# Scoring the end keys of a block-sparse attention step in 32-query tiles

## The chip, the cores and the metric

The kernel runs on one core of a Trainium2 chip. The metric is the device time of one execution in microseconds; for the kernel before it is known from three runs.

## What is computed

Two stages are joined. The first is attention over 4 batches, 8 heads, 768 positions and 64 dimensions, in blocks of 32 positions. A query block sees its own block and the two neighbours, the first and the last block of the sequence (the *end keys*), and three blocks drawn at random for it; the queries of the first and the last block see everything. In the reference:

```
mask = np.abs(blk_i - blk_j) <= window
mask = mask | (blk_i == 0) | (blk_j == 0) | (blk_i == n_blocks - 1) | (blk_j == n_blocks - 1)
for qb in range(n_blocks):
    for kb in sampled_blocks[qb]:
        mask[qb * block:(qb + 1) * block, kb * block:(kb + 1) * block] = True
```

Softmax over the masked scores and the product with the values follow. The second stage is a mixture of 8 experts with noisy top-2 routing: each of the 3072 rows goes through two experts, `relu(x @ w1) @ w2`, weighted by the gate.

## The kernel before, in words

Attention runs as a list of steps (`Attention.macros`). Two batches lie together (`bb`), two heads of a pair lie on the two halves of the 128 partitions (`a`), and a step takes one batch, four heads (two head pairs `r` times `a`) and 128 queries. There are 40 G steps (four ordinary query blocks of 32 in each: 2 batch pairs, 5 units, 4 steps a unit) and, for the queries of the first and last block and the two blocks left over, 8 X steps and 16 D steps. A G step has 256 keys for each query block `j`: 96 sampled keys and 96 neighbours (the *windows*, one matmul of 192 columns for each `j`), and 64 end keys between them.

`Attention.scores` (line 207) gives these to TensorE. The operands are fp32, and each fp32 matmul appears in the trace as two passes, each with a weight load. For each head pair `r`, lines 227 to 229 score the end keys of all 128 queries at once: for each `a` one matmul on a tile of 64 rows by 128 columns (64 by 64 in an X step), 64 columns moving. Lines 230 to 239 then score the windows: for each `j` and `a` one matmul on a tile of 64 rows by 32 columns, 192 columns moving. So a G step issues 8 instructions of the first kind and 32 of the second, an X step 8 and 16. Every result goes to the PSUM tile `s`.

The order on TensorE is fixed in `steps` (line 433). In step n: scores of n; transposes of n-1 (line 299); router work on rows that are done (`turn` line 544, `logits` line 556, and others) at three spots; the product with the values of step n-2 (`av`, line 314, 64 instructions on tiles of 128 by 32). VectorE takes the maximum of the scores (`top`, line 246) and the negative bias `nb` (line 265), ScalarE the exponentials (line 287).

The sampled keys come by GpSimd: `gather_k` (line 205) copies 12 blocks of 32 columns out of the resident keys, for one batch of a unit, two steps before their first use. In the same queue stand the gathers of the sampled values, `gather_v` (line 189, an indirect DMA), each behind a small copy to `tick` (line 417) that waits for VectorE's latest maximum. The neighbouring values come by ScalarE's queue (line 182). Instructions are read from memory by DMA queues of their own.

Of the kernel before, what the change touches and what calls it, by code (L numbers as in the profile page):

```python
# [18 lines left out]
P = 128  # L19
# [19 lines left out]
class Attention:  # L39
# [167 lines left out]
    def scores(self, m):  # L207
        kind, k, bb, h, kh = m
        nc = self.nc
        hpair, g = self.units[k]  # L210
        S = self.st["s", m] = self.ps_s.tile([P, 2, 512], F32, name="s")
        q, KT = self.st["q", k][:, bb], self.KT[hpair][:, bb]
        f = self.first(g)
        hp = lambda a: slice(64 * a, 64 * a + 64)
        mm = lambda out, l, r, pos: nc.tensor.matmul(out, l, r, start=True, stop=True, tile_position=pos)  # L215
        if kind == "D":
            for r in range(2):
                for a in range(2):
                    pr, o = 2 * h + r, 64 * (1 - r)
                    mm(S[o:o + 64, a, 0:384], q[hp(a), pr, 64:P], KT[hp(a), pr, 384 * kh:384 * kh + 384], (64 * a, o))  # L220
            return
        own = self.kv[hpair][:, bb * self.BW:(bb + 1) * self.BW]
        ends = lambda x, n: x.rearrange("p (n c) -> p n c", c=32)[:, 0:n:n - 1, :]
        for r in range(2):
            pr = 2 * h + r
            col, js, o0, n = (256 * r, range(4), 0, P) if kind == "G" else (0, range(2), 64 * r, 64)
            for a in range(2):
                out = S[o0:o0 + n, a, col + 96:col + 160].rearrange("p (n c) -> p n c", c=32)
                mm(out, q[hp(a), pr, 0:n], ends(KT[hp(a), pr], self.NB), (64 * a, o0))
            for j in js:  # L230
                for a in range(2):
                    o = o0 + 32 * j
                    at = own[hp(a), (j * self.PR + pr) * 96:]
                    win = self.GW + pr * self.S + 32 * (f + j - 1)
                    rhs = bass.AP(tensor=at.tensor, offset=at.offset,
                                  ap=[list(at.ap[0]), [win - (j * self.PR + pr) * 96, 2], [1, 96]])
                    out = S[o:o + 32, a, col:col + 256].rearrange("p (n c) -> p n c", c=32)
                    out = bass.AP(tensor=out.tensor, offset=out.offset, ap=[list(out.ap[0]), [160, 2], [1, 96]])
                    mm(out, q[hp(a), pr, 32 * j:32 * j + 32], rhs, (64 * a, o))
# [1111 lines left out]
```

## Time and profile before

| | |
|---|---|
| median of three runs | 897.31 us |
| lowest, highest | 894.2, 899.99 us |
| profiled execution, first to last instruction | 898.7 us |
| mean granted TensorE clock | 0.983 |
| attention's matmuls | 8.5 to about 323 us |
| experts | from 323.95 us |

The profile is of one execution on the chip; its span is in the third line of the table, and no other time is shown for that execution. A busy TensorE is not TensorE at its peak: matmuls overlap, and their ends are modelled. Idle time is printed with what ended it; "issue" means that the engine waited for nothing that the profile shows. Rows that give a stretch list, for each engine, busy microseconds and the number of instructions, then the granted clock, the DMA share and GB/s.

### The profile page before, as it was taken

Reading aid. Unit: us, or ns where it says so; the run is one execution under the profiler, and the core shown is the slowest. Engines: PE = TensorE matmul, PEld = TensorE weight load, DVE = VectorE, ACT = ScalarE, POOL = GpSimd, SP = SyncE. Lnnn points to the kernel's source line nnn. Section 1 sums busy time; section 2 is a strip of 40 time slices with the busy share of each in tenths; the row PEclk is TensorE's granted clock in tenths of the full one; section 3 lists DMA queues with packets and bytes.
Section 4 is the critical chain, followed back from the end, with each engine's and each line's share of the span. In section 5 each row is a group of like instructions: output and inputs, shape, how many; then the busy total and the mean of one; then the engine's idle time right before and its main releaser. Section 6 shows DMA issues by size and latency. Waiting matters only on the chain.

```text
span 898.7 us, 21745 instructions
## 1 busy us (share of the span) xinstructions
PE 827.7 (92%) x9033; PEld 491.8 (55%) x9033; DVE 404.9 (45%) x924; ACT 295.2 (33%) x570; POOL 299.9 (33%) x550
## 2 busy tenths in 40 slices
PE   4999889898996897989999999999999999999993
PEld 2667656766675675465545545545545545545541
DVE  3545557567567557413343343343343343342420
ACT  2565545454565443112212312212212302311300
POOL 2545444441344400233423423413423423424020
PEclk9999999999998899999999999999999999999997
DMA  8856796792568868393952943962952942943011
GB/s 338 297 179 210 228 277 200 284 316 67 153 173 229 215 180 308 123 215 73 221 204 76 266 137 65 199 224 65 217 205 74 268 160 65 270 141 101 9 37 38
DMA packets 122618, 159.70 MB, mean 178 GB/s; under 512 B 66581, under 2 KB 83221, under 8 KB 122512
## 3 DMA queue, kind: packets, MB, share of 16 engines
q1 hardware_dynamic: 96400, 75.76, 31.3%
q0 software_dynamic: 17616, 57.47, 22.1%
q10 hardware_dynamic: 8496, 25.01, 8.9%
q8 instruction: 73, 1.20, 0.6%
q14 instruction: 33, 0.27, 0.1%
HBM read 117.30 MB, written 27.10 MB: 161 GB/s over the span
## 4 chain that ended last, share of the span: by engine, by line
PE 52%; DMA 3%; issue 2%; DVE 0%; POOL 0%; SPq 0%; POOLq 0%
PE ph L891 27%; PE py L913 22%; PE py L924 2%; DMA out_dram<-y,mt 2%; DMA xtb<-xg 1%; DMA xg<-x_rows,gi 0%; PE py L933 0%; POOL out_dram L964 0%; SPq L846 0%; DVE y L962 0%; DVE y L958 0%; PE pr L945 0%; DVE o_ex L1057 0%; POOLq L980 0%; POOLq L964 0%
## 5 line engine op out<-in xcount | busy, mean ns | idle before, releaser
L896 ACT ACTIVATE hh<-ph 128x408 f16<-128x408 f32 (+2 forms) x136 | 66.6, 492 | 368.1 <-PE ph L891 271.7
L964 POOL DMA_INDIRECT out_dram<-y,mt x56 | 61.5, 1098 | 340.6 <-DVE y L958 149.1
L913 PE MATMUL py<-w2h,hh 128*128 128x512 f16 x384 | 145.6, 379 | 0.0
L913 PE MATMUL py<-w2l,hh 128*128 128x512 f16 x384 | 145.5, 379 | 0.0
L913 PE MATMUL py<-w2h,hl 128*128 128x512 f16 x384 | 145.5, 379 | 0.0
L897 DVE SCALAR_TENSOR_TENSOR hl<-ph,hh 128x408 f16<-128x408 f32 (+2 forms) x136 | 75.9, 560 | 153.4 <-ACT hh L896 133.0
L215 PE MATMUL s<-kv,q 64*32 64x192 f32 (+3 forms) x1920 | 114.1, 349 | 20.4 <-DMA kv<-in_k_dram 8.5
L913 PEld LDWEIGHTS <-hh 128*128 128x128 f16 x768 | 74.5, 98 | 90.2 <-issue 2.5
L891 PE MATMUL ph<-xta,w1hb 128*128 128x408 f16 x512 | 109.4, 336 | 0.8 <-issue 0.8
L958 DVE SCALAR_TENSOR_TENSOR y<-py,r_tab,pv 128x512 f32<-128x512 f32 (+1 forms) x49 | 36.7, 750 | 152.0 <-PE py L913 146.6
L891 PE MATMUL ph<-xtb,w1ha 128*128 128x408 f16 (+1 forms) x448 | 93.4, 329 | 5.5 <-DMA xtb<-xg 4.2
L301 ACT ACTIVATE t<-t 128x512 f32<-128x512 f32 (+1 forms) x120 | 62.6, 566 | 96.3 <-PE t L299 93.7
L215 PEld LDWEIGHTS s<-kv,q 64*32 64x32 f32 (+2 forms) x1920 | 53.2, 124 | 60.9 <-issue 32.3
L205 POOL COPY kv<-kv 128x128 f32 x264 | 67.2, 301 | 52.9 <-issue 22.1
L891 PEld LDWEIGHTS <-w1ha 128*128 128x128 f16 x576 | 56.7, 99 | 44.0 <-issue 5.8
L830 POOL DMA_INDIRECT xg<-x_rows,gi x56 | 62.1, 1109 | 51.4 <-DVE gi L816 35.8
L287 ACT ACTIVATE p<-s,nb 128x256 f32<-128x256 f32 x176 | 69.4, 476 | 19.8 <-DVE nb L265 14.6
L246 DVE TENSOR_REDUCE nm<-s 128x4 f32<-128x1024 f32 (+1 forms) x48 | 54.4, 1133 | 44.1 <-PE s L215 34.0
L891 PEld LDWEIGHTS <-w1hb 128*128 128x128 f16 x512 | 50.1, 98 | 39.3 <-issue 1.1
L299 PE MATMUL t<-ident,p 128*128 128x128 f32 x448 | 66.2, 290 | 2.1 <-ACT t L301 2.1
L891 PE MATMUL ph<-xta,w1lb 128*128 128x408 f16 x256 | 65.1, 336 | 0.0
L299 PEld LDWEIGHTS t<-ident,p 128*128 128x128 f32 x448 | 50.1, 145 | 24.7 <-issue 16.4
(176 smaller groups left out, 1013.7 us busy)
## 6 DMA issues: line engine op xcount, KB each, us to landing
wraw<-in_moe_w_dram SPq DMA_DIRECT2D x64, 512.0 KB
vb<-in_v_windows_dram ACTq DMA_DIRECT2D x28, 390.0 KB
vb<-in_v_windows_dram ACTq DMA_DIRECT2D x14, 520.0 KB
kv<-in_v_dram SPq DMA_DIRECT2D x4, 1560.0 KB
q<-in_q_dram SPq DMA_DIRECT2D x12, 512.0 KB
kv<-in_k_dram SPq DMA_DIRECT2D x8, 768.0 KB
out_dram<-zero ACTq DMA_DIRECT2D x8, 768.0 KB
x_rows<-x SPq DMA_DIRECT2D x20, 256.0 KB
```

The lines of the kernel that those rows point to most:

```text
L205: nc.gpsimd.tensor_copy(KG[:, j, :, 32 * s:32 * s + 32], KT[:, :, bass.ds(offs[3 * j + s], 32)])
L215: mm = lambda out, l, r, pos: nc.tensor.matmul(out, l, r, start=True, stop=True, tile_position=pos)
L246: red = lambda out, x: nc.vector.tensor_reduce(out, x, axis=AX.X, op=ALU.max, negate=True)
L287: self.nc.scalar.activation(p[:, 256 * u:256 * u + 256], S[:, a, 256 * r:256 * r + 256], AF.Exp, bias=nb[:, u:u + 1], scale=0.125)
L299: self.nc.tensor.transpose(T[i][:, c:c + P], p[:, i * w + c:i * w + c + P], self.ident)
L301: self.nc.scalar.activation(t[:, i * w:(i + 1) * w], T[i][:, 0:w], AF.Copy)
L830: g = nc.gpsimd.indirect_dma_start(out=self.xg[0:m, c], out_offset=None, in_=self.x_dram[0:nr], in_offset=bass.IndirectOffsetOnAxis(ap=r[" ...
L891: nc.tensor.matmul(ph[:, b, 0:m], w[wt][:, kb, fs], r["xt"][:, kb, a, o:o + m], start=i == 0, stop=i == last)
L896: nc.scalar.activation(hv, ph[:, b, 0:m], AF.Relu)
L897: nc.vector.scalar_tensor_tensor(self.hl[:, f, o:o + m], ph[:, b, 0:m], 0.0, hv, op0=ALU.max, op1=ALU.subtract)
L913: nc.tensor.matmul(py, h[:, f, o], w[x][:, f, :], start=i == 0, stop=i == last)
L964: nc.gpsimd.indirect_dma_start(out=self.out, out_offset=bass.IndirectOffsetOnAxis(ap=r["mt"][0:m, c:c + 1], axis=0), in_=y[0:m], in_offset ...
```

## The change

The end keys of a step are scored for each block of 32 queries by itself: for each `j` and `a` one matmul on a tile of 64 rows by 32 columns, with 64 columns moving, into the same places of `s`. The shape of the tile is that of the windows' matmuls, which follow unchanged. A G step's end keys take 32 instructions on 8 tiles for both pairs together where there were 8 on 2 (4 and 16 for each pair), an X step's 16 where there were 8; the weight loads are as many again.

```
-            col, js, o0, n = (256 * r, range(4), 0, P) if kind == "G" else (0, range(2), 64 * r, 64)
-            for a in range(2):
-                out = S[o0:o0 + n, a, col + 96:col + 160].rearrange("p (n c) -> p n c", c=32)
-                mm(out, q[hp(a), pr, 0:n], ends(KT[hp(a), pr], self.NB), (64 * a, o0))
+            col, js, o0 = (256 * r, range(4), 0) if kind == "G" else (0, range(2), 64 * r)
+            for j in js:
+                o = o0 + 32 * j
+                for a in range(2):
+                    out = S[o:o + 32, a, col + 96:col + 160].rearrange("p (n c) -> p n c", c=32)
+                    mm(out, q[hp(a), pr, 32 * j:32 * j + 32], ends(KT[hp(a), pr], self.NB), (64 * a, o))
             for j in js:
                 for a in range(2):
```

## Rows read from the trace of the kernel before

**Rows 1.** The page: engines, the instruction queue, the chain that ended last.
```profile
PE 827.7 (92%) x9033; PEld 491.8 (55%) x9033; DVE 404.9 (45%) x924; ACT 295.2 (33%) x570; POOL 299.9 (33%) x550
...
q8 instruction: 73, 1.20, 0.6%
...
PE 52%; DMA 3%; issue 2%; DVE 0%; POOL 0%; SPq 0%; POOLq 0%
```

**Rows 2.** Busy time by stretch: PE, PEld, DVE, ACT, POOL, clock, DMA share, GB/s.
```profile
46.66:69.03 22.37, 20.98 (x506) 15.02 (x509) 11.05 (x23) 13.28 (x31) 10.70 (x31) 1.00 0.62 196
69.03:203.01 133.98, 120.62 (x2796) 89.49 (x2789) 81.35 (x248) 71.44 (x163) 61.74 (x186) 0.99 0.79 250
...
244.77:319.10 74.33, 63.97 (x1388) 48.26 (x1387) 48.12 (x140) 40.37 (x89) 33.02 (x88) 0.91 0.78 207
```

**Rows 3.** The same by stretch, line 215 alone.
```profile
69.03:203.01 133.98, 51.31 (x928) 25.60 (x928) 0.99 0.79 250
244.77:319.10 74.33, 25.00 (x480) 12.96 (x480) 0.91 0.78 207
```

**Rows 4.** TensorE's timeline where the experts begin: start, length, instruction.
```profile
323.95 0.70 PE L891 MATMUL ph<-xta,w1ha 128*128 128x320 f16 x4
```

**Rows 5.** Line 215: idle time until the copies came (us, times).
```profile
  POOL kv L205: 12.5, 28
```

**Rows 6.** GpSimd's timeline, 148 to 160 us; idle time before in brackets.
```profile
148.99 0.18 POOL L417 COPY tick<-nb 1x1 f32<-1x1 f32 x1 [4.75 <-DVE nb L265]
...
152.68 3.20 POOL L205 COPY kv<-kv 128x128 f32 x12 [1.82 <-DMA vb<-in_v_windows_dram]
```

**Rows 7.** TensorE's timeline, 90 to 94 and 116.8 to 125 us.
```profile
93.02 0.92 PE L215 MATMUL s<-kv,q 64*128 64x64 f32 x19 [1.78 <-issue]
...
119.19 0.26 PE L314 MATMUL po<-va,t 128*32 128x65 f32 x3 [1.51 <-issue]
...
124.70 0.32 PE L314 MATMUL po<-vb,t 128*32 128x65 f32 x8 [0.63 <-issue]
```

**Rows 8.** Busy time by stretch, between such stops, and one without.
```profile
93.01:119.17 26.16, 23.40 (x505) 17.63 (x504) 14.41 (x32) 15.00 (x35) 13.52 (x44) 0.93 0.81 234
119.17:124.69 5.52, 4.89 (x126) 3.90 (x127) 3.37 (x11) 2.21 (x5) 0.17 (x1) 1.00 0.76 203
124.69:131.04 6.35, 5.21 (x127) 3.65 (x126) 4.89 (x31) 3.55 (x10) 4.02 (x15) 1.00 0.95 317
...
147.89:152.26 4.37, 4.37 (x142) 3.36 (x135) 4.09 (x16) 2.56 (x6) 1.21 (x2) 1.00 0.61 195
```

**Rows 9.** DMA queues (packets, MB, share): 69.03:203.01, 119.17:122, 121.9:123.4 and 147.89:150.
```profile
q8 instruction: 22, 0.36, 1.1%
...
q0 software_dynamic: 160, 0.55, 70.6%
...
q8 instruction: 1, 0.02, 4.7%
...
q8 instruction: 1, 0.02, 3.9%
```

**Rows 10.** Busy time by stretch, line 215: ends, then windows, one pair.
```profile
148.45:148.82 0.37, 0.36 (x4) 0.30 (x4) 1.00 0.25 50
148.82:149.31 0.48, 0.48 (x18) 0.18 (x16) 1.00 0.00 0
```

**Rows 11.** TensorE's timeline, the product with the values.
```profile
151.76 0.30 PE L314 MATMUL po<-vb,t 128*32 128x65 f32 x8
151.87 0.30 PE L314 MATMUL po<-va,t 128*32 128x65 f32 x8
```

**Rows 12.** Busy time by stretch, line 215, X step: ends, windows, one pair.
```profile
209.19:209.46 0.27, 0.26 (x4) 0.20 (x5) 1.00 0.23 62
209.46:209.91 0.46, 0.46 (x12) 0.15 (x8) 1.00 0.00 0
```

**Rows 13.** Busy time by stretch, behind the stop that ends at 93.02.
```profile
93.00:96.50 3.50, 3.48 (x35) 2.77 (x37) 1.53 (x2) 1.39 (x3) 2.88 (x12) 0.66 1.03 261
```

## The prediction

> **What bounds the kernel now.** I read the page first: TensorE is busy 92% of the span, the chain that ended last is half matmul time, and a DMA queue of its own carries instructions: 73 packets, 1.20 MB, so 16.4 KB each. With 9033 matmuls and 9033 weight loads that is about 250 TensorE instructions to a packet [rows 1]. Then the busy time by stretch: the changed lines run only in the attention stage, of which the stretches from 46.66 to 319.10 us hold all 40 G steps: 5, 23 and 12 of them in the first, second and fourth stretch (928 and 480 matmul instructions of the line in the second and fourth, 40 to a G step, and 8 of the 928 are a D step's; 5 are left for the first) [rows 2, 3]. The experts' first matmul starts right behind the last logits, with no idle time before it [rows 4], so what the attention stage gains or loses should move everything after it.
>
> Inside the stage two things besides TensorE's own work set the pace. **The gathered keys**: TensorE waited 28 times, 12.5 us in all, for GpSimd's copies of the sampled key blocks [rows 5], four waits to such a step. GpSimd may begin only after a reduction's result (its tick), then starts a gather, and then copies for 3.20 us; in the example the tick is at 148.99 and the copies end at 155.88 [rows 6]. **Instruction fetch**: TensorE also stops in the middle of groups whose operands are all there, with no semaphore named: 1.78 us before 93.02, 1.51 before 119.19, 0.63 before 124.70 [rows 7]. From one such stop to the next TensorE issues 1009, 253 and 253 matmuls and loads [rows 8]: multiples of one packet. In the 5.52 us chunk that ends at 124.70, no instruction packet moves up to 122.0, while the software gather queue takes 70.6% of the engines' time; then one does [rows 9]. So one packet is fetched while one is used, it queues behind the value gathers, and some 2.6 us pass from its start to the first use. That the fetch is one packet ahead only is my reading of these rows.
>
> **The change, part by part.**
> Removed and added, TensorE's own time: a G step today takes 0.37 us for a 64x128 group of ends and 0.48 us for a 64x32 group of windows, and both again for the second head pair: 1.70 us [rows 10]. Afterwards there is one shape throughout. The nearest row for back-to-back 32-column tiles in fp32 is the values' product: rounds of 8 instructions on four tiles (two passes of 65 columns each) follow each other every 0.11 us [rows 11]. So two passes of 64 columns cost 0.11 us, and two of 192 columns 0.11 x 192/65 = 0.33 us; what a windows group takes beyond this, 0.48 - 0.33 = 0.15 us, is filling and draining, and falls once a step, not four times. New step: 2 x (0.11 + 0.33) + 0.15 = 1.03 us, so 0.67 less. The other bound: each ends group still pays its own 0.15 us, (0.11 + 0.15 + 0.48) x 2 = 1.48, so 0.22 less. I take 0.67, since nothing of another shape stands between. Over 40 steps 26.8 us (bound: 8.8). An X step takes 2 x (0.27 + 0.46) = 1.46 us [rows 12]; by the same sum it becomes 1.03, 8 x 0.43 = 3.4 us. Together up to 30.2 us of TensorE time.
>
> What does not move: the tick, gather, copies, reduction, exps and every DMA stay where they are in program order. No wait is added.
>
> What of this saving the gathered keys keep: in the 28/4 = 7 steps that wait for copies, the step ends by the copies' end plus the last windows tile and the second pair. That remainder goes from 0.48 + 0.37 + 0.48 = 1.33 us to 0.33 + 0.11 + 0.33 + 0.15 = 0.92, so 0.41 less, in place of the 1.34 that the two steps spanned by the copy chain would give. If nothing else waited: 7 x 0.41 + 13 x 1.34 = 20 us for the 20 pairs of steps, and about 15 if the reductions, which share VectorE with the router, keep a third of the second term (an estimate); with 2.5 us from the X steps, -17 to -22.
>
> What the added instructions cost: a G step's scores go from 40 matmul instructions and 40 loads to 64 and 64, that is 48 more; an X step's by 16. TensorE has 5585 instructions in the 23-step stretch and 22 packets moved there [rows 2, 9], 254 per chunk, 134.0/22 = 6.09 us per chunk. After: (5585 + 23 x 48)/254 = 26.3 chunks. How long a fetch takes in itself: two neighbouring chunks that were paced by it alone took 5.52 and 6.35 us, mean 5.94 [rows 8]. A quiet one is at most 4.37 us, a chunk passed without a stop [rows 8]; with its packet moving within 2.1 us of the chunk's start [rows 9] I take 3.2. Weighted by the DMA share of 0.79 [rows 2]: 0.79 x 5.94 + 0.21 x 3.2 = 5.36 us. Then the fetch alone needs 26.3 x 5.36 = 141.0 us where the stretch now takes 134.0. The quiet 21%, 5.5 chunks, are paced by TensorE at about 4.0 us (a step of 3.7 us for 300 instructions is 3.2 per chunk, with some waiting), 0.8 more each: 4.4. Sum 145.4, **+11 us**. Ends: -1 if a fetch takes 4.9 us on average, since its queueing differs with each packet's place among the gathers; +19 if the 8 us of other waits, which the same sum leaves over today (22 x (0.79 x 5.94 + 0.21 x 4.9) = 126 of 134), come on top.
> First stretch (DMA share 0.62 [rows 2]): 5 steps, 0.62 x 5.94 + 0.38 x 3.2 = 4.9 us a fetch, (1015 + 240)/254 = 4.9 chunks, 24 us against 22.4 by fetch, 19.0 by TensorE: I take -1 (-3.4 to +1.8). Fourth stretch: (2775 + 576)/254 = 13.2 chunks x 5.3 = 70 us against 74.3, where other waits remain: -2 (-8 to +6). X steps: -2.5 (-3.4 to 0).
> The granted clock: after the 1.78 us stop it is 0.66 for 3.50 us [rows 13], between its 1.2 and 2.4 GHz levels; such a dip loses about 1.5 us. With more and longer stops I add one or two dips, +2 (0 to +8).
> Sum: +11 - 1 - 2 - 2.5 + 2 = **+7.5 us**. The trace's execution spans 898.7 us, 1.4 above the median of 897.3 and inside the runs' 894.2 to 899.99; against the median: 905 us.
>
> **Rivals.**
> *The fetch keeps up* (faster). If the fetch can run further ahead than I read, or its queueing shrinks, TensorE's saving counts, cut by the copies: -17 to -22 us where all of it comes through, less where some stops stay, so 876 to 888. For it: most packet boundaries pass today without a stop. Against: the stops at multiples of a packet, and 20% more instructions in less time.
> *A draw*. The fetch paces the times of heavy gathers and TensorE the quiet ones, and what the one loses the other gains: 891 to 902. The ends of my terms allow it.
> *The small tiles don't overlap* (the change doesn't do what it says). If 16 short matmuls take as long as the 0.37 us of the group that they replace [rows 10], TensorE saves nothing and the longer fetch remains; the quiet chunks then stay near today's 4.9 us, 5.5 x 0.9 = 5 us more, and the X and first-stretch gains of 3.5 go: 914 us. Against: the values' rounds pass an instruction each 14 ns [rows 11]. The Trainium skill has the rule (TensorE: Matmul & The Clock Gate, "Wait — 56ns, not 53.3ns?"): starts never come closer than about 25 ns however few the columns. By it 16 matmuls need 0.40 us, more than the group replaced. The rounds on different tiles contradict it here.
>
> **How the numbers follow.** About 1% (9 us) is what a measurement of this kernel can tell from no change. Forecast, paced by fetch, +2 to +20: 0.53, of which 0.36 lies above +9. Serialised tiles: 0.07, all slower. Draw: 0.19, of which 0.04 faster. Fetch keeps up: 0.21, of which 0.18 faster. So slower 0.43, same 0.35, faster 0.22. The range takes in the forecast's and draw's ends and half of the fast case: 883 to 920; the forecast's own is 899 to 917.
>
> **What would show it.** In the changed kernel's trace: 81 instruction packets instead of 73; a G step's scores near 1.0 us where nothing stops them; more stops without a named semaphore, spaced by 250 instructions, in the stretch that is now 69 to 203 us; fewer waits for the key copies. I am wrong on the fetch if the number of such stops does not rise, and wrong on the tiles if an undisturbed step's scores take 1.5 us or more.

## The result, and the profile after

The changed kernel takes 902.38 us (median of 20 runs, 896.51 to 907.73) against 897.83 us for the kernel before (20 runs beside them): a ratio of 1.0077, 95% interval 1.0055 to 1.0099. Slower by 0.8%: 6.9 us by the ratio, which sets runs beside each other, 4.6 between the medians; +7.5 was forecast, and 905 us. It lies under the bound of 1% that the prediction set for telling a change from none in a few runs; over 20 the interval is clear of none. The profiled execution took 904.83 us and spans 903.1 us.

The page of the changed kernel, the lines that answer to [rows 1]:

```profile
PE 809.3 (90%) x10057; PEld 493.1 (55%) x10057; DVE 405.2 (45%) x924; ACT 294.6 (33%) x570; POOL 299.0 (33%) x550
...
q8 instruction: 81, 1.33, 0.6%
...
PE 51%; DMA 3%; issue 2%; DVE 0%; POOL 0%; SPq 0%; POOLq 0%
```

TensorE is busy 18 us less, with 1024 matmuls and 1024 loads more, and the instruction packets are 81, as forecast. The busy time did not fall off the end: the experts begin later, at 331.34 us where [rows 4] had 323.95, again with no idle time in between (TensorE's timeline):

```profile
331.34 1.13 PE L893 MATMUL ph<-xta,w1ha 128*128 128x320 f16 x3
```

Cut at the first G step, at the second block of D and X steps and at the G steps behind it, the attention stage of the kernel before has these stretches (columns as in [rows 2]):

```profile
46.66:201.07 154.41, 139.66 (x3264) 103.19 (x3263) 91.23 (x265) 83.16 (x190) 71.11 (x214) 0.99 0.77 245
201.07:244.77 43.70, 39.69 (x678) 27.68 (x671) 29.83 (x90) 22.17 (x49) 10.15 (x27) 1.00 0.35 100
244.77:323.95 79.18, 68.20 (x1532) 52.07 (x1532) 50.98 (x149) 41.65 (x91) 33.02 (x88) 0.91 0.75 198
```

and that of the changed kernel these:

```profile
47.20:211.00 163.80, 129.84 (x3940) 106.12 (x3939) 90.10 (x260) 81.54 (x187) 70.86 (x214) 0.92 0.72 228
211.00:254.70 43.70, 37.93 (x714) 27.00 (x715) 30.93 (x95) 22.84 (x50) 10.43 (x28) 0.96 0.39 112
254.70:331.33 76.63, 61.25 (x1820) 49.58 (x1820) 51.13 (x149) 41.05 (x91) 34.48 (x89) 0.93 0.81 203
```

The first 28 G steps lose 9.4 us although TensorE is busy 9.8 us less in them; the last 12 gain 2.6; the D and X steps between gain nothing. Over the three stretches TensorE's busy time falls by 18.5 us and its idle time, the stretch less the busy time, rises by 25.4, from 29.7 to 55.1. An undisturbed G step's scores, TensorE's timeline from the first score to the first transpose (1.70 us in [rows 10], both pairs):

```profile
50.61 1.26 PE L215 MATMUL s<-kv,q 64*32 64x64 f32 x64
51.81 1.09 PE L301 MATMUL t<-ident,p 128*128 128x128 f32 x8
```

1.20 us. And inside it, line 215 alone, the first pair's windows and then the second pair's ends:

```profile
50.75:51.07 0.32, 0.32 (x32) 0.31 (x33) 1.00 0.96 247
51.07:51.18 0.11, 0.11 (x31) 0.11 (x14) 1.00 0.92 378
```

0.32 and 0.11 us (the counts hold instructions that are still in flight from the group before): the 16 matmuls of the ends pass in 0.11 us, 7 ns each, on eight tiles side by side. So TensorE does save 0.50 us in an undisturbed step, and something gives back more. What TensorE waited for in the attention stage without a semaphore, in the kernel before (line, waited for: us in total, times, longest):

```profile
PE po L314 <- issue: 9.5, 12, 2.3
...
PE s L215 <- issue: 2.4, 4, 1.8
```

and in the changed kernel:

```profile
PE s L215 <- issue: 19.8, 14, 4.1
PE po L316 <- issue: 11.7, 8, 3.9
PE pe L637 <- issue: 4.0, 1, 4.0
PE t L301 <- issue: 3.5, 2, 1.9
...
PE pe L558 <- issue: 1.8, 2, 1.2
```

11.9 us became 40.8. TensorE's timeline shows such stops, in the answer to [rows 7]:

```profile
73.75 0.24 PE L316 MATMUL po<-vb,t 128*32 128x65 f32 x1 [2.40 <-issue]
...
110.58 0.33 PE L316 MATMUL po<-va,t 128*32 128x65 f32 x4 [3.91 <-issue]
...
124.36 0.26 PE L316 MATMUL po<-va,t 128*32 128x65 f32 x3 [2.05 <-issue]
```

The stretches between neighbouring stops again hold one packet of instructions each, as in [rows 8], and now they follow one another:

```profile
73.74:77.95 4.21, 3.67 (x127) 3.16 (x127) 2.40 (x5) 1.72 (x3) 0.11 (x1) 1.00 0.34 130
77.95:81.78 3.83, 2.75 (x127) 2.25 (x128) 1.29 (x6) 1.57 (x4) 1.16 (x2) 1.00 0.69 184
81.78:87.17 5.39, 3.86 (x127) 3.12 (x126) 3.50 (x7) 3.17 (x7) 4.76 (x16) 1.00 0.62 157
87.17:93.80 6.63, 4.27 (x126) 3.40 (x127) 2.33 (x6) 2.54 (x6) 2.77 (x7) 1.00 0.99 296
```

Counting every 256th instruction of TensorE through the attention stage (from the start of the instruction ahead of it, waits on semaphores included), 7 stops of over 0.45 us stood at a packet's first instruction before, and 25 do now. All 25 come 2.3 to 3.3 us after the start of their packet's transfer. GpSimd's copies are waited for less, 7.2 us in 16 times where [rows 5] had 12.5 in 28: GpSimd's work is the same, so most likely TensorE comes to the copies later.

One stop shows what the packet waits behind. The chunk that starts at 102.82 us runs dry at 106.7; the DMA queues from 102.83 to 107.9 us:

```profile
q1 hardware_dynamic: 178, 1.00, 61.2%
q10 hardware_dynamic: 132, 0.48, 33.1%
q0 software_dynamic: 1, 0.00, 0.3%
```

No instruction packet; in the 1.4 us behind it there is one, and 110.58 is 2.7 us after its earliest start:

```profile
q8 instruction: 1, 0.02, 5.3%
```

What delays a packet shows over all chunks of this stage. Where the DMA engines were over 90% busy with other transfers from a chunk's first instruction to the next packet's transfer, that transfer began 3.3 us after the chunk in the median (26 chunks, 0.7 to 5.9 us); where they were under 20% busy, 1.1 us (11 chunks).

Of the 7.4 us at the experts' begin, 3.0 come back behind it: there two waits, for a router result (2.1 to 1.0 us) and for gathered rows (4.2 to 2.6), are shorter by 2.7 together. The spans differ by 4.4.

### The profile page after: what moved, and what is told of

Same layout as the page of the kernel before. It is cut to its first block, busy times and chain, and to the rows that moved or that the text cites. A ratio compares the mean times of both kernels' runs of the same rounds, so it can differ in the third digit from the quotient of the medians.

```text
span 903.1 us, 23793 instructions
## 1 busy us (share of the span) xinstructions
PE 809.3 (90%) x10057; PEld 493.1 (55%) x10057; DVE 405.2 (45%) x924; ACT 294.6 (33%) x570; POOL 299.0 (33%) x550
## 4 chain that ended last, share of the span: by engine, by line
PE 51%; DMA 3%; issue 2%; DVE 0%; POOL 0%; SPq 0%; POOLq 0%
PE ph L893 27%; PE py L915 22%; PE py L926 2%; DMA out_dram<-y,mt 2%; DMA xtb<-xg 1%; PE py L935 0%; DMA xg<-x_rows,gi 0%; POOL out_dram L966 0%; SPq L848 0%; DVE y L964 0%; DVE y L960 0%; PE pr L947 0%; DVE o_ex L1059 0%; POOLq L982 0%; POOLq L966 0%
## 5 line engine op out<-in xcount | busy, mean ns | idle before, releaser
L966 POOL DMA_INDIRECT out_dram<-y,mt x56 | 59.3, 1058 | 339.3 <-DVE y L960 148.8
L215 PE MATMUL s<-kv,q 64*32 64x192 f32 (+2 forms) x2944 | 85.9, 307 | 37.1 <-issue 19.8
L215 PEld LDWEIGHTS s<-kv,q 64*32 64x32 f32 (+1 forms) x2944 | 45.9, 114 | 55.7 <-issue 35.0
L301 PE MATMUL t<-ident,p 128*128 128x128 f32 x448 | 69.4, 298 | 7.4 <-ACT t L303 3.9
```

The lines of the kernel that those rows point to most:

```text
L301: self.nc.tensor.transpose(T[i][:, c:c + P], p[:, i * w + c:i * w + c + P], self.ident)
L966: nc.gpsimd.indirect_dma_start(out=self.out, out_offset=bass.IndirectOffsetOnAxis(ap=r["mt"][0:m, c:c + 1], axis=0), in_=y[0:m], in_offset ...
```

## The experiments

The theory: TensorE's instructions come in packets of 256, one at a time, each behind whatever the DMA queues hold; the change raises the number of instructions in a G step by a fifth, and this costs more than the tiles save. The rivals: the new tiles are slow in themselves; only TensorE's own time counts; the key copies or VectorE pace the steps. The stops in the table are those at a packet's first instruction, counted as above; the kernel before has 7.

| kernel | change to the time of the kernel before beside it (95%) | packets | matmuls in a G step's scores | stops |
|---|---|---|---|---|
| the change | +0.77% (0.55 to 0.99) | 81 | 64 | 25 |
| the change again | +0.40% (0.05 to 0.76) | 81 | 64 | 22 |
| g_only | +1.46% (0.88 to 2.04) | 80 | 64 | 17 |
| x_only | +0.44% (0.08 to 0.80) | 73 | 40 | 6 |
| ends_first | -0.50% (-1.01 to 0.00) | 73 | 40 | 8 |
| ends_first_x | -0.42% (-0.84 to 0.00) | 73 | 40 | 8 |
| extra | +3.13% (2.07 to 4.18) | 80 | 64 | 8 |
| light_before | -1.85% (-2.86 to -0.85) | 73 | 40 | 4 |
| light_after | -1.83% (-3.00 to -0.66) | 81 | 64 | 15 |
| x_phase | +1.20% (-0.09 to 2.49) | 75 | 40 | 7 |
| one_pass_new | -1.03% (-1.37 to -0.68) | 75 | 48 | 8 |
| one_pass_old | -1.69% (-2.45 to -0.94) | 71 | 36 | 11 |
| one_pass_first | -1.75% (-2.33 to -1.17) | 71 | 36 | 10 |

**One part alone: g_only.**

```
-            for a in range(2):
...
+            small = kind == "G"
+            for i in js if small else range(1):
+                for a in range(2):
+                    o, w = (o0 + 32 * i, 32) if small else (o0, n)
...
```

> Only the G steps score their end keys in 32-query tiles; the X steps keep the 64x64 tiles. Theory (instruction fetch paces the stage): the G steps bring 1920 of the 2048 added instructions, so about 25 stops at packet boundaries as with the whole change (7 before), and the whole loss and more: 3 to 12 us above the kernel before. Rival (TensorE's own time alone): 40 steps x 0.4 to 0.5 us less, 16 to 20 us below it. Rival (the small tiles are slow in themselves): above it, with no more stops than before.

915.46 us against 903.42. The G steps carry the whole loss and more, 12.0 us between the medians and 13.2 by the ratio, at or past the upper end of what was expected; stops without a semaphore were 33.4 us in its attention stage, and 17 stops, not 25, stood at packets' starts. The rival that only TensorE's own time counts is out. With the next one the parts do not add up: 1.46% and 0.44% apart, 0.77% together.

**The other part alone: x_only**, the same edit with `kind == "X"`.

> Only the X steps score their end keys in 32-query tiles. Theory: 128 instructions more, half a packet, where fetches are hardly waited for; an X step's scores take 0.62 us in the changed kernel's trace in place of 1.44, so 8 x 0.8 = 6.6 us less at most, some of it hidden in the first four: 2 to 6 us below the kernel before, stops unchanged at about 7. Rival (small tiles are slow in themselves): no gain.

907.43 us against 903.42: a miss. The stretches of its profiled execution say where:

```profile
45.70:202.90 157.20, 143.04 (x3264) 105.64 (x3263) 91.11 (x265) 83.05 (x190) 71.70 (x215) 0.96 0.75 241
202.90:244.40 41.50, 36.45 (x709) 26.18 (x704) 29.66 (x90) 21.80 (x48) 10.10 (x26) 1.00 0.36 106
244.40:331.80 87.40, 76.28 (x1532) 57.96 (x1532) 51.34 (x149) 41.79 (x91) 34.83 (x89) 0.82 0.66 179
```

The X steps' own stretch is 2.2 us shorter, as expected. The G steps, whose code is that of the kernel before, lost 2.8 and 8.2 us, with a granted clock of 0.96 and 0.82 where it was 0.99 and 0.91. The loss lies in TensorE's busy time: the same 3264 and 1532 matmuls took 3.4 and 8.1 us longer than in the kernel before, while stops without a semaphore came to 13.2 us against 11.9. The lower clock is not the profiled execution's alone: over the ten runs its mean was 0.964, over those of the kernel before beside them 0.973. So a loss of this size can come without any more stops. The 64 instructions that each block of X steps adds move the packets' starts to other places in the G steps behind; whether that is the cause, the next was to tell.

**x_phase**: x_only with 12 one-column matmuls in each X step, so that the packets' starts move by a whole packet.

```
+        if kind == "X":
+            for i in range(12):
+                a, o = i % 2, 32 * (i // 2 % 4)
+                mm(S[o:o + 32, a, 0:1], q[hp(a), 2 * h, o:o + 32], KT[hp(a), 2 * h, 0:1], (64 * a, o))
```

> x_only with 12 one-column matmuls more in every X step, so that each block of four X steps holds 4 x 64 = 256 instructions more than in the kernel before, one packet, and the packets begin at the same instructions of the G steps as in the kernel before. If x_only was slower because its 64 instructions move the packets' starts to other places of the following G steps, this one is back at the kernel before or 1 to 4 us below it; if the X steps' tiles or noise were the cause, it stays 2 to 6 us above.

908.55 us against 901.29, the interval from just below none to 2.5%: not back at the kernel before. The place of the packets' starts is not supported as the cause. The last G stretch of its profiled execution is again long by busy time, at a clock of 0.80:

```profile
243.08:328.81 85.73, 76.40 (x1533) 58.60 (x1532) 51.24 (x149) 41.54 (x91) 33.66 (x88) 0.80 0.67 182
```

What draws the clock down there stays open.

**The shapes without the instructions: ends_first.** One loop scores the ends of both head pairs, in the old tiles, and a second one then the windows of both:

```
-        for r in range(2):
...
+        for r, (col, js, o0, n) in enumerate(places):
...
+        for r, (col, js, o0, n) in enumerate(places):
...
```

> The old tiles, but the ends of both head pairs ahead of the windows of both, so a step changes the shape once instead of three times, with no instruction more. By the model of 0.15 us per fill and drain, a G step saves 0.3 us of TensorE time, 12 us in all. Theory: packets stay 73, stops stay near 7 to 10, and half or more of the saving is kept: 4 to 10 us below the kernel before. Rival (the gathered keys or VectorE pace the steps, TensorE's time doesn't matter): within 2 us of it.

898.64 us against 903.42, at the low end of what was expected and just at the edge of being told from none. A step's scores take 1.41 us (TensorE's timeline, first score to first transpose):

```profile
51.00 1.47 PE L215 MATMUL s<-kv,q 64*128 64x64 f32 x40
52.41 0.44 PE L301 MATMUL t<-ident,p 128*128 128x128 f32 x2
```

The edit reorders the X steps too, and takes an X step's scores from 1.44 to 0.76 us:

```profile
205.93 0.83 PE L215 MATMUL s<-kv,q 64*64 64x64 f32 x24
206.69 0.33 PE L301 MATMUL t<-ident,p 128*128 128x128 f32 x1
```

So 0.29 us a G step and 0.68 us an X step, 17 us of TensorE time, bring some 4 us with no instruction added; the change brought 0.50 us a G step, and cost 4.6 to 6.9.

**Both: ends_first_x.** The two edits above together.

> As the one before it (ends of both pairs first, old tiles in G steps), and X steps in 32-query tiles. Theory: the two gains add, 6 to 15 us below the kernel before. Rival (something else paces the stage): no better than the better of the two parts alone.

898.55 us against 903.42, no better than ends_first, where the theory expected the gains to add. The test could hardly show it: with ends_first's order the X steps are already at 0.76 us, and the small tiles take them to 0.60, 1.3 us over eight steps.

**Instructions without work: extra.**

```
+            if kind == "G" and r == 0:
+                for i in range(12):
+                    a, o = i % 2, 32 * (i // 2 % 4)
+                    mm(S[o:o + 32, a, 256:257], q[hp(a), pr, o:o + 32], KT[hp(a), pr, 0:1], (64 * a, o))
```

> The kernel before, and in every G step 12 matmuls of one column (24 instructions and 24 loads, as many as the change adds) between the first pair's windows and the second pair's ends; what they write is overwritten. Theory: packets go to about 80, stops at packet boundaries from 7 to 18 or more, and the time rises by 10 to 22 us, more than by the change, since nothing is saved on TensorE. Rival (instructions cost only their time on TensorE, 24 pairs at 7 to 14 ns, 0.17 to 0.34 us a step): 7 to 13 us more with stops still near 7.

928.64 us against 901.29. It is more than either expected, and not by the mechanism that I named: 8 stops stood at packets' starts, hardly more than the 7 of the kernel before, and stops without a semaphore come to 23.2 us, not to the 40.8 of the change, since TensorE took longer over each packet itself. The windows and the 24 one-column matmuls behind them take 0.35 + 0.37 us (line 215 alone, first pair), where [rows 10] has 0.48 for the windows, so an undisturbed step takes 0.24 us more, 40 x 0.24 = 9.6 us, and the granted clock of the first G stretch falls to 0.83:

```profile
102.59:102.94 0.35, 0.35 (x18) 0.35 (x24) 1.00 0.06 24
102.94:103.31 0.37, 0.37 (x39) 0.36 (x18) 1.00 0.03 11
```

```profile
46.50:228.10 181.60, 165.45 (x3936) 135.03 (x3935) 91.78 (x265) 83.26 (x189) 71.52 (x214) 0.83 0.66 209
```

In that stretch TensorE's busy time is 25.8 us above the kernel before, its idle time 1.4. So it was no clean test of the fetch, and as many instructions more did not by themselves bring more stops.

**Without the value loads: light_before and light_after.** In both, `gather_v` and `load_v` return without a transfer for the later units:

```
+        if k > 2:
+            return
```

> The kernel before, without the loads of sampled and neighbouring values from the third unit after the first on (34 of the gathers and as many window loads fall away; the product uses old values). Both theories: faster than the kernel before, 10 to 40 us, since waits for copies and packets shrink. Theory: stops at packet boundaries only up to about 85 us, 3 or fewer behind it. The comparison is with the next kernel.

> The changed kernel, without the same loads of values. Theory (the packets wait behind the value loads; without these TensorE's saving comes through): faster than light_before by 8 to 18 us, with few stops at packet boundaries behind 85 us. Rival (the small tiles or their number are slow in themselves, whatever the DMA queues hold): slower than light_before by about as much as the change, 3 to 8 us.

883.14 and 884.07 us, ratios to the kernel before of 0.9815 and 0.9817. The gain of 8 to 18 us that the theory expected did not come. With four runs each the two differ by 0.3 us in the mean, give or take 6, so a loss of some us is not excluded: that the loss of the change hangs on these transfers is suggested and not shown. From 85 to 186 us TensorE is busy 9 us less in the changed one, with no time won, by the first row below of light_before and the second of light_after (its first G stretch is 4.5 us longer, the two behind it 2.0 and 4.8 shorter):

```profile
85.00:186.00 101.00, 95.83 (x2387) 73.20 (x2384) 69.74 (x220) 60.01 (x137) 31.93 (x136) 1.00 0.35 118
```

```profile
85.00:186.00 101.00, 86.51 (x2739) 70.66 (x2739) 67.34 (x191) 57.92 (x133) 32.78 (x137) 0.97 0.35 119
```

Stops without a semaphore are still 19.8 us in light_after (5.6 in light_before), with loads of keys, queries and rows left in the queues. Full queues are not needed for a stop: in light_after no other transfer ran from the chunk's first instruction at 88.40 us to its packet at 89.87, the packet was used 2.7 us later, and the chunk still ended in a stop of 0.47 us. The theory holds here by half.

**Fewer instructions in the new tiles: one_pass_new.** The upper half of an fp32 word read as bf16 needs one pass, not two:

```
-        ends = lambda x, n: x.rearrange("p (n c) -> p n c", c=32)[:, 0:n:n - 1, :]
+        ends = lambda x, n: x.bitcast(BF16).rearrange("p (n c t) -> p n c t", c=32, t=2)[:, 0:n:n - 1, :, 1]
+        top16 = lambda x: x.bitcast(BF16).rearrange("p (c t) -> p c t", t=2)[:, :, 1]
...
-                    mm(out, q[hp(a), pr, 32 * j:32 * j + 32], ends(KT[hp(a), pr], self.NB), (64 * a, o))
+                    mm(out, top16(q[hp(a), pr, 32 * j:32 * j + 32]), ends(KT[hp(a), pr], self.NB), (64 * a, o))
```

> The changed kernel once more, on the chip of the next three: 3 to 8 us above the kernel before, about 25 stops at packet boundaries.

> The changed kernel, with the end keys' products taken from the upper halves of the fp32 words (bf16, one pass in place of two): the same tiles, as many of them, half the instructions for the ends. A G step has 80 + 16 = 96 instructions and loads for its scores, 16 more than before in place of 48. Theory (the number of instructions is what costs): about 3 packets more than before in place of 8, stops at packet boundaries 8 to 15 in place of 25, and TensorE's saving of about 0.6 us a step comes through in part: 4 to 14 us below the kernel before. Rival (32-query tiles or the mixing with windows are what costs, by the clock or else): as slow as the changed kernel, 3 to 8 us above the kernel before.

On one chip: the change 901.55 us, one_pass_new 886.82, the kernel before 896.19. The scores of a step take 1.05 us against 1.20 (48.97 to 50.02 in TensorE's timeline), which is 6 us over 40 steps; the kernel is 14.7 us faster.

```profile
48.97 1.11 PE L215 MATMUL s<-kv,q 64*32 64x64 bf16 x48
50.02 1.09 PE L302 MATMUL t<-ident,p 128*128 128x128 f32 x8
```

Stops without a semaphore in the attention stage fall from 37.7 us in the change again to 16.7 in one_pass_new, and those at packets' starts from 22 to 8:

```profile
PE po L316 <- issue: 17.3, 9, 3.7
PE s L215 <- issue: 16.5, 13, 2.7
PE pe L637 <- issue: 3.5, 1, 3.5
...
PE t L301 <- issue: 0.4, 1, 0.4
```

```profile
PE po L317 <- issue: 12.4, 6, 3.5
...
PE pe L559 <- issue: 2.2, 1, 2.2
PE pe L547 <- issue: 2.1, 1, 2.1
```

and the first G stretch from 162.3 us to 148.8, at nearly the same granted clock, 0.91 and 0.92:

```profile
45.70:208.00 162.30, 132.04 (x3936) 105.98 (x3935) 89.75 (x260) 81.80 (x187) 70.65 (x214) 0.91 0.72 230
45.60:194.40 148.80, 126.61 (x3492) 98.77 (x3491) 91.78 (x266) 83.19 (x190) 73.70 (x216) 0.92 0.80 255
```

Of these 13.5 us TensorE's busy time gives 5.4 and its idle time 8.1. So neither the 32-query tiles, nor their mixing with the windows, nor a low clock by itself need make a kernel slower than the one before: same tiles, same order, nearly the same clock, a quarter of the scores' instructions less. The operands of the ends are bf16 here, so the arithmetic differs too.

**And in the old tiles: one_pass_old.** The same lambdas in the kernel before.

> The kernel before with the same single-pass ends in its own 64x128 tiles: 8 instructions and loads fewer in a G step, no tile changed. Theory: one packet less, about 0.1 us a pair and 8 us of TensorE time less, stops near 7: 3 to 9 us below the kernel before. Against one_pass_new this says what the new tiles are worth once the instructions differ by 24 a step and not by 48.

880.55 us against 896.19, 15.6 us below where 3 to 9 were expected. Its scores take 1.24 us a step (49.76 to 51.00), 0.19 more than one_pass_new, and yet it ends 6 us earlier, with 24 instructions a step less and 71 packets against 75:

```profile
49.76 1.31 PE L215 MATMUL s<-kv,q 64*128 64x64 bf16 x36
51.00 1.09 PE L300 MATMUL t<-ident,p 128*128 128x128 f32 x8
```

The two intervals overlap (0.9863 to 0.9932, 0.9755 to 0.9906), the runs hardly do (882.12 to 894.38, 875.30 to 884.23). Against the kernel before, a G step saves 0.46 us (1.70 to 1.24), nearly the 0.50 of the change, with 8 instructions (matmuls and loads) fewer in place of 48 more. Here most of the saving came through: 40 x 0.46 = 18.4 us, and 15.6 gained, with 11 stops at packets' starts against 7. That contrast, the same saving with and without added instructions, is the plainest that the runs give.

**All together: one_pass_first**, the single-pass ends in old tiles and ahead of both pairs' windows.

> Single-pass ends in the old tiles, and the ends of both pairs ahead of the windows of both: the fewest instructions and two changes of shape fewer in a step. Theory: the best of all, 7 to 16 us below the kernel before, with stops near 7. Rival (the copies of the keys, VectorE or the clock pace the steps by now): no better than ends_first, 3 to 6 us below.

879.89 us against 896.19, -1.75%: as far down as one_pass_old and no further, so no gain of the reordering shows on top. Both beat both kernels, with the end keys' operands cut to bf16; with the arithmetic kept, ends_first and ends_first_x are the only ones that may.

## Why the prediction was right, point by point

The way it went and the mechanism, stops of TensorE at packets' starts, were foreseen. That the sum came so near is in part luck. In the G stretches the fetch, less TensorE's saving, was forecast at +8 us. There 6.8 were measured, but some 3.3 of them are matmuls that took longer, the term of the clock, forecast at +2; and the X steps brought 0.0 in place of -2.5. These errors cancel.

**TensorE's own time**: the direction was right, both sizes were off. The G step went from 1.70 to 1.20 us, not to 1.03: the ends and the first windows take the 0.11 and 0.33 us of the working, but the last windows group takes about 0.63 (the rest of the 1.20), 0.30 us beyond its 0.33 in place of the 0.15 that I read out of the old groups. The X step went to 0.64 us, not 1.03, since the two pairs use different tiles and ran side by side (from 242.99 to the transpose at 243.63 us):

```profile
242.99 0.70 PE L215 MATMUL s<-kv,q 64*32 64x64 f32 x32 [0.32 <-ACT p L280]
243.63 0.88 PE L301 MATMUL t<-ident,p 128*128 128x128 f32 x6
```

Together 40 x 0.50 + 8 x 0.82 = 26.6 us, forecast 30.2.

**Instruction fetch**: the step that carried the sign. The first two stretches were forecast at +11 and -1 and came to +9.4 us together, with the clock's part inside it; the last was forecast at -2 and came to -2.6. That more instructions cost idle time is shown by one_pass_new against the change again, and by one_pass_old, which keeps a saving of the same size. extra shows the condition: it adds as many instructions, but TensorE takes longer over each packet, and the stops do not grow. Of the sum, the 3.7 us of a step for 300 instructions stands in none of the rows. That a packet is fetched one at a time is a reading that the traces agree with: in the changed kernel, between 45 and 331 us, each chunk but two holds the start of one packet's transfer. The two, one with two starts and one with none, lie between 216 and 242 us, where the packets at 224.43 and 232.47 us began 0.1 and 0.5 us before the next chunk. What was wrong in it: the packet does not wait behind the value gathers of the software queue alone. At 102.8 to 107.9 us it was the two hardware queues, with 94% of the engines' time between them; and with the value loads gone the stops did not go. Nor did the forecast see that a chunk in the new tiles can be used up before a packet comes that waits for nothing (the chunk at 88.40 us of light_after).

**X steps**: forecast -2.5 us, measured 0.0 in their second block. x_only gained 2.2 there. In the changed kernel TensorE is busy 1.8 us less in that block and idle 1.8 us more; its waits for VectorE and ScalarE there are longer, the longest for a router result (1.2 us).

**Copies**: the forecast of fewer waits for them held, 12.5 to 7.2 us.

**The clock**: 0.99 to 0.92 in the first stretch, more than the one or two dips that I counted, and such a dip loses 1.2 us by [rows 13] (3.50 us at 0.66), not 1.5. How much of the loss it made can be set against the busy time. The 40 G steps and the four X steps in the three stretches save 40 x 0.50 + 4 x 0.82 = 23.3 us, and TensorE's busy time fell by 18.5. So 4.8 us are matmuls that took longer, 4.2 of them in the first stretch (28 x 0.50 = 14.0 saved, 9.8 measured), the one where the clock fell furthest. Without them the added idle time of 25.4 us would about match the saving. So the stops took the saving away, and the lower clock probably made most of what was lost beyond it; no run isolates the clock.

**The rivals**: serialised tiles, and the 25 ns between starts that the Trainium skill gives (TensorE: Matmul & The Clock Gate, "Wait — 56ns, not 53.3ns?"), are out for the ends' tiles: 16 matmuls in 0.11 us. The one-column matmuls of extra, at 0.37/24 = 15.6 ns, lie below that figure as well. *The fetch keeps up* would have needed the stops to stay; they grew from 11.9 to 40.8 us. *A draw* was forecast up to 902 us, and 902.38 were measured, a loss just under the bound of 1%; by the time alone the two can't be told apart, and the 25 stops speak for the forecast's mechanism.

## What to carry to other kernels

Before splitting a matmul into more, smaller ones, count the engine's instructions in a step against the time that its packets take to come: here TensorE's own work on 256 instructions was some 4 us (129.84 us for 7879 in the first stretch), and with the DMA queues full it took up to 8.3 us from one packet's first instruction to the next one's. An idle engine whose wait names nothing, at even distances in instructions, is the mark of it. One pass in place of two, in the same tiles, brought 14.7 us of which only 6 were TensorE's own; in the old tiles nearly the whole saving came through. And look at the busy time beside the idle time: x_only and extra lost in matmuls that took longer, at a lower granted clock, and not in stops.

## What the runs showed of the hardware that I had not expected

An instruction packet comes late behind the hardware queues' loads as it does behind the software gathers (5.1 us without a packet, ahead of the stop before 110.58). A stretch with many one-column matmuls was granted 0.83 of the clock, the lowest of all first stretches, with TensorE busy for 165 of 181.6 us. And x_only lost 11 us in G steps that it does not change, at clocks of 0.96 and 0.82; what drew the clock down is left open.
